# Late modulation vectors as VectorE dot products, and feed-forward transfers in program order, in a fused transformer block

## The chip, the cores and the metric

The kernel runs on one core of a Trainium2 chip (trn2). The metric is the device time of one execution in microseconds. The kernel before took 1283.59 us (median of 3 runs, 1283.0 to 1285.08).

## The reference, cut to what matters

```python
mod = (silu(c) @ w_mod).reshape(1, 6, 1, 1024)        # w_mod is 1024 x 6144, bf16
sa, ca, ga, sb, cb, gb = ...                           # six vectors of 1024
h = layernorm(x) * (1 + ca) + sa                       # x is 2048 x 1024
x = x + ga * attention(h)                              # 32 heads of 128, window of 512 keys, wq, wo
h = layernorm(x) * (1 + cb) + sb
x = x + gb * (silu(h @ w_gate) * (h @ w_up)) @ w_down  # feed-forward width 3584
```

`sa` and `ca` are needed at once. The other four vectors are needed later: `ga` and `gb` as rows that are the same in all partitions, `cb` and `sb` as columns (one value per partition). These four are the "late modulation vectors".

## The kernel before

The program is a list of 128 head steps (4 chunks of 512 rows, 32 heads each), with small tasks hung on the steps by `at(k, ...)`, and then the feed-forward (FFN) stage. A scheduler orders each engine's instructions; `pin` holds an instruction to program order. `fetch` and `load` issue all transfers from one queue, that of SyncE (SPq).

The late vectors were made on TensorE, two vectors at a time. The stationary side is silu(c), widened to 32 equal columns:

```python
sil32 = const.tile([P, DT, 32], BF16, name="sil32")
for dt in range(DT):                                   # eight VectorE fills, in the startup
    nc.vector.tensor_scalar(out=sil32[:, dt, :], in0=ones_bf[:, 0:32],
                            scalar1=siluc[:, dt:dt + 1], scalar2=None, op0=ALU.mult)

def mod_rows(n, part):                                 # runs at steps 5, 13, 21 and 29
    ps = mm("row_ps")
    tiles = [wm_rows.pop(0) for _ in range(2)]
    for k in range(4):
        for i in range(4):
            nc.tensor.matmul(ps[32 * i:32 * i + 32, :], lhsT=sil32[:, 4 * part + k, :],
                             rhs=tiles[i // 2][:, k, (i % 2) * 512:(i % 2 + 1) * 512],
                             start=(k == 0), stop=(k == 3))
    # ... VectorE adds the two parts and the result goes to DRAM as row_d

def load_cols(n, k, dst, add_one):                     # cb1 at step 16
    src = row_d[n][k:k + 2, :].rearrange("a (b p) -> p (a b)", p=P)
    with nc.allow_non_contiguous_dma(reason="1024 values to columns"):
        fetch(out=dst, in_=src)
    if add_one:                                        # VectorE, waits for that load
        nc.vector.tensor_scalar(out=dst, in0=dst, scalar1=1.0, scalar2=None, op0=ALU.add)
```

In the FFN stage transfers are not pinned, so the scheduler may order them freely:

```python
stage.update(dma=False, steps=False)
for cc in range(NTC):
    for fg in range(NFG):
        if (cc, fg) != (0, 0):
            load_gu(cc, fg)                            # gate and up tiles of this group
        if cc > 0:
            load_wd(cc, 0, fg)
        # ... emit_gu and the remaining tasks
    # ... down projection; its wd tiles are loaded in front of it
```

## Time and profile before

| | before |
|---|---|
| time, median of 3 | 1283.59 us |
| span of the profiled run | 1283.0 us |
| TensorE (PE) busy | 1270.0 us, 99% |
| VectorE (DVE) busy | 577.3 us, 45% |
| DMA queue of SyncE | 54.1% of 16 engines |

The first lines of the profile page of the kernel before; each engine line is busy time, share of the span, and instructions.

```profile
span 1283.0 us, 18137 instructions
PE 1270.0 (99%) x7601; PEld 643.1 (50%) x7601; DVE 577.3 (45%) x1271; ACT 333.9 (26%) x433; POOL 1.2 (0%) x8
```

TensorE hardly rests, so only work taken off it, or one of its few waits, can shorten the run. The groups view of the kernel before shows the two kinds of work that the change trades. Its columns are line, engine, operation, tiles and shapes, count; then busy time in us and mean ns of one; then idle time before.

```profile
L779 PE MATMUL row_ps<-wmr,sil 128*32 128x512 bf16 x64 | 4.2, 382 | 0.0
L955 DVE SCALAR_TENSOR_TENSOR junk<-wq 128x1024 bf16<-128x1024 bf16 x32 | 38.9, 1215 | 0.0
L955 DVE DVE_READ_ACCUMULATOR junk<-wq 128x1 f32 x32 | 2.6, 82 | 0.0
```

The 64 narrow matmuls occupy TensorE for 4.2 us together, although each record is 382 ns long. The timeline of TensorE shows one group of 16 (start, duration, instruction):

```profile
46.55 1.05 PE L779 MATMUL row_ps<-wmr,sil 128*32 128x512 bf16 x16
```

It takes 1.05 us, where 16 ordinary 128x512 matmuls at 0.216 us would take 3.46 us. The second and third lines of the groups view are a dot product that the kernel already does elsewhere: 1215 + 82 ns for 128x1024.

Four lines of the waits view of the kernel before turn out to matter. Columns: who waited, on whom; us in total, times, longest.

```profile
DVE modT L802 <- DMA modT<-row_d: 3.6, 1, 3.6
PE a_ps L1096 <- DVE acc L1102: 1.0, 1, 1.0
PE gu_ps L1173 <- DVE guT L1179: 0.8, 1, 0.8
PE mod_ps L753 <- DMA wm<-in_w_mod_dram: 1.7, 1, 1.7
```

The third stands in the FFN stage, and the fourth is TensorE waiting in the startup for a load of `w_mod`; both come back below. The first two belong together. This is VectorE in the timeline of the kernel before, from 86 to 94 us (start, duration, instruction; in brackets the idle time before it and what ended it):

```profile
87.84 0.54 DVE L835 TENSOR_SCALAR xn<-x,mv 128x1024 bf16<-128x1024 bf16 x1
92.00 0.17 DVE L802 TENSOR_SCALAR modT<-modT 128x8 f32<-128x8 f32 x1 [3.62 <-DMA modT<-row_d]
92.08 0.69 DVE L816 BATCH_NORM_STATS2 st<-x 128x6 f32<-128x512 bf16 x1
92.69 0.67 DVE L1102 COPY acc<-a_ps 128x512 f32<-128x512 f32 x1
```

And this is the chain of waits of the kernel before across the same time (start, duration, what):

```profile
86.93 5.05 DMA modT<-row_d
...
92.77 0.60 DVE acc L1102
...
93.41 1.89 PE a_ps L1096 x8
```

The `+ 1` on the cb columns (L802) stands in VectorE's order and waits 3.6 us for a 4 KB load that took 5.05 us. The accumulator copy behind it (L1102) comes late, and TensorE's next `a_ps` group waits for it.

### The profile page before, as it was taken

What the parts mean: (1) busy time and instruction counts of PE and PEld (TensorE: products, weight loads), DVE (VectorE), ACT (ScalarE), POOL (GpSimd) and SP (SyncE); (2) the same over time, 40 slices, a digit from 0 to 9 for tenths busy, and PEclk for the clock granted to TensorE, in tenths of its full rate; (3) what the DMA queues carried; (4) which work ended last, traced back from release to release, by engine and by line L of the source; (5) the groups of instructions that cost most, each with busy time, mean ns of one, the idle gap of its engine ahead of it and who ended that gap; (6) DMA issues with size and microseconds to landing.
All of it is one profiled execution on the core that took longest, in us unless ns stands there. A gap on an engine that the chain in (4) does not pass through costs nothing.

```text
span 1283.0 us, 18137 instructions
## 1 busy us (share of the span) xinstructions
PE 1270.0 (99%) x7601; PEld 643.1 (50%) x7601; DVE 577.3 (45%) x1271; ACT 333.9 (26%) x433; POOL 1.2 (0%) x8
## 2 busy tenths in 40 slices
PE   8999999999999999999999999999999999999998
PEld 4555555555555555555554444444444444444444
DVE  4464557865577755576663642221212221221122
ACT  3543334343333433333341111011100111011100
POOL 0000000000000000000000000000000000000000
PEclk8999999999999999999999999999999999999999
DMA  9878566557355554445678484454536455454401
GB/s 286 275 187 234 169 149 171 133 142 204 98 124 156 148 140 148 116 149 131 132 195 247 129 249 149 139 189 147 180 103 218 140 164 164 135 193 134 129 22 47
DMA packets 280108, 204.21 MB, mean 159 GB/s; under 512 B 113865, under 2 KB 273609, under 8 KB 280018
## 3 DMA queue, kind: packets, MB, share of 16 engines
q1 hardware_dynamic: 275106, 198.78, 54.1%
q10 hardware_dynamic: 4912, 4.20, 1.0%
q8 instruction: 61, 1.00, 0.3%
q14 instruction: 29, 0.24, 0.1%
HBM read 174.08 MB, written 4.21 MB: 139 GB/s over the span
## 4 chain that ended last, share of the span: by engine, by line
PE 96%; DMA 2%; DVE 1%; SPq 0%; ACT 0%; issue 0%; DVEq 0%
PE gu_ps L1173 29%; PE a_ps L1096 17%; PE q_ps L1019 17%; PE d_ps L1193 15%; PE o_ps L1064 9%; PE s_ps L1032 8%; DMA wm<-in_w_mod_dram 1%; DMA hT<-xn 1%; PE q_ps L940 0%; DMA modT<-row_d 0%; PE row_ps L779 0%; SPq L664 0%; PE mod_ps L753 0%; DVE st L816 0%; ACT pT L1034 0%; PE h_ps L927 0%
## 5 line engine op out<-in xcount | busy, mean ns | idle before, releaser
L1034 ACT ACTIVATE pT<-s_ps 128x1024 bf16<-128x1024 f32 x256 | 248.7, 1020 | 341.8 <-PE s_ps L1032 341.8
L1096 PE MATMUL a_ps<-wo,oT 128*128 128x512 bf16 x1024 | 241.9, 379 | 1.0 <-DVE acc L1102 1.0
L1019 PE MATMUL q_ps<-hT,wq 128*128 128x512 bf16 x1000 | 236.7, 379 | 0.3 <-DVE modT L755 0.3
L1173 PE MATMUL gu_ps<-hT,wg 128*128 128x512 bf16 x896 | 211.7, 379 | 0.8 <-DVE guT L1179 0.8
L1179 DVE TENSOR_TENSOR guT<-gu_ps,sg 128x512 bf16<-128x512 f32 x112 | 77.4, 691 | 282.5 <-ACT sg L1178 282.5
L1178 ACT ACTIVATE sg<-gu_ps 128x512 bf16<-128x512 f32 x112 | 66.9, 597 | 489.6 <-PE gu_ps L1173 438.4
L1193 PE MATMUL d_ps<-wd,guT 128*128 128x512 bf16 (+2 forms) x952 | 194.2, 366 | 0.0
L916 DVE CAST qT<-q_ps 128x512 bf16<-128x512 f32 x128 | 88.2, 691 | 176.9 <-PE q_ps L1019 176.3
L1173 PE MATMUL gu_ps<-hT,wu 128*128 128x512 bf16 x672 | 163.3, 379 | 0.0
L1096 PEld LDWEIGHTS <-oT 128*128 128x128 bf16 x1024 | 99.9, 98 | 122.3 <-issue 2.1
L1019 PEld LDWEIGHTS <-wq 128*128 128x128 bf16 x1000 | 97.8, 98 | 117.8 <-issue 0.3
L1193 PEld LDWEIGHTS <-guT 128*128 128x128 bf16 x952 | 90.9, 98 | 103.0
L1064 PEld LDWEIGHTS <-pT 128*128 128x128 bf16 x2048 | 126.6, 98 | 30.6 <-issue 0.4
L1173 PEld LDWEIGHTS <-wg 128*128 128x128 bf16 x896 | 87.6, 98 | 106.5 <-issue 1.1
L1064 PE MATMUL o_ps<-v_sb,pT 128*128 128x130 bf16 x2048 | 137.1, 220 | 0.0
L1032 PE MATMUL s_ps<-qT,kT 128*128 128x512 bf16 x512 | 131.5, 379 | 0.6 <-ACT pT L1034 0.6
L1173 PEld LDWEIGHTS <-wu 128*128 128x128 bf16 x672 | 65.8, 98 | 79.3
L1051 DVE TENSOR_TENSOR oq<-o_ps,rl 128x256 bf16<-128x256 f32 (+2 forms) x256 | 101.2, 419 | 4.3
L1197 DVE TENSOR_TENSOR f<-d_ps,gb_bc 128x512 f32<-128x512 f32 (+2 forms) x34 | 22.4, 660 | 147.1 <-PE d_ps L1193 147.1
L1104 DVE TENSOR_TENSOR acc<-a_ps,acc 128x512 f32<-128x512 f32 x64 | 44.0, 688 | 38.8 <-PE a_ps L1096 38.8
L1032 PEld LDWEIGHTS <-kT 128*128 128x128 bf16 x512 | 44.9, 98 | 31.7 <-issue 1.3
L1173 PE MATMUL gu_ps<-hT,v_sb 128*128 128x512 bf16 x224 | 57.5, 379 | 0.0
(77 smaller groups left out, 372.6 us busy)
## 6 DMA issues: line engine op xcount, KB each, us to landing
wq<-in_A_wq_dram SPq DMA_DIRECT2D x64, 512.0 KB, 4.2
wo<-in_A_wo_dram SPq DMA_DIRECT2D x64, 512.0 KB, 5.7
wg<-in_B_w_gate_dram SPq DMA_DIRECT2D x56, 512.0 KB, 4.5
wd<-in_B_w_down_dram SPq DMA_DIRECT2D x56, 512.0 KB, 7.1
wu<-in_B_w_up_dram SPq DMA_DIRECT2D x42, 512.0 KB, 5.9
wmr<-in_w_mod_dram SPq DMA_DIRECT2D x8, 1024.0 KB, 11.5
v_sb<-in_B_w_up_dram SPq DMA_DIRECT2D x14, 512.0 KB, 6.2
x<-in_A_x_dram SPq DMA_DIRECT2D x16, 256.0 KB, 5.7
```

The source lines that it names most:

```text
L916: nc.vector.tensor_copy(out=t, in_=q_ps)
L1019: nc.tensor.matmul(q_ps, lhsT=wq_tiles[(cc, h // 4, dt // 4)][:, dt % 4, (h % 4) * P:(h % 4 + 1) * P], rhs=hT[("h1", cc)][:, dt, :], start ...
L1032: nc.tensor.matmul(s_ps[:, i, :], lhsT=kT[:, kv, j * P:(j + 1) * P], rhs=qT[g], start=True, stop=True)
L1034: nc.scalar.activation(out=p[:, 2 * jj:2 * jj + 2, :], in_=s_ps, func=ACT.Exp, scale=scale)
L1051: nc.vector.tensor_tensor(out=dst, in0=ps[:, s0:s0 + cnt, 0:Dh], in1=sc, op=ALU.mult)
L1064: nc.tensor.matmul(o_slot["ps"][:, s_, :], lhsT=pT[g][:, j, t * P:(t + 1) * P], rhs=v_sb[:, kv, j, 0:VN], start=(j == 0), stop=(j == WT - 1))
L1096: nc.tensor.matmul(a_ps, lhsT=oT[(cc, 2 * q + i)][:, hh % 4, t * P:(t + 1) * P], rhs=wo_tiles[(cc, q, dh, i)][:, hh % 4, :], start=(hh == ...
L1104: nc.vector.tensor_tensor(out=acc[(cc, t)][:, dsl], in0=a_ps, in1=acc[(cc, t)][:, dsl], op=ALU.add)
L1173: nc.tensor.matmul(ps[:, n, :], lhsT=gu_w[(cc, fg, nm, dt // 4)][:, dt % 4, fi * P:(fi + 1) * P], rhs=hT[("h2", cc)][:, dt, :], start=(dt ...
L1178: nc.scalar.activation(out=g, in_=ps[:, 0, :], func=ACT.Silu)
L1179: nc.vector.tensor_tensor(out=guT[(cc, fg)][:, fi, :], in0=ps[:, 1, :], in1=g, op=ALU.mult)
L1193: nc.tensor.matmul(d_ps, lhsT=guT[(cc, f // 4)][:, f % 4, t * P:(t + 1) * P], rhs=wd_tiles[(cc, dh, f // 4)][:, f % 4, c0:c0 + w], start=( ...
```

## The change

Each late vector is computed on VectorE. Columns of `w_mod` are loaded by a transposing DMA (128 columns x 1024 rows per load), so that a vector element is the dot product of one partition's row with silu(c), which is spread over all partitions once (`c_bc`). There are 32 such tiles, one every second head step. The 64 narrow matmuls, the fills of `sil32`, the row loads, and the column load with its `+ 1` go. In the FFN stage the transfers are pinned to program order, and the next group's gate and up tiles are asked for before the wd tiles.

```diff
-    sil32 = const.tile([P, DT, 32], BF16, name="sil32")
-    for dt in range(DT):
-        nc.vector.tensor_scalar(out=sil32[:, dt, :], in0=ones_bf[:, 0:32],
-                                scalar1=siluc[:, dt:dt + 1], scalar2=None, op0=ALU.mult)
     # ... (load_rows, mod_rows, load_gate, load_cols removed)
+    c_d = dp.tile([DT, P], BF16, name="c_d", tag="c_d", bufs=1)
+    c_bc = const.tile([P, D], BF16, name="c_bc")
     # ...
+    def load_wmT(vec, j):
+        if j % 4 == 0:
+            wm_cols[(vec, j // 4)] = hpool.tile([P, 4, D], BF16, name="wmT", tag="hT")
+        c0 = vec * D + j * P
+        pin(nc.sync.dma_start_transpose(out=wm_cols[(vec, j // 4)][:, j % 4, :],
+                                        in_=w_mod[:, c0:c0 + P]), "dma")
+
+    def mod_dot(vec, j, dst):
+        t = wm_cols[(vec, j // 4)]
+        junk = wk.tile([P, D], BF16, name="junk", tag="junk", bufs=1)
+        pin(nc.vector.scalar_tensor_tensor(out=junk, in0=t[:, j % 4, :], scalar=1.0, in1=c_bc,
+                                           op0=ALU.mult, op1=ALU.mult,
+                                           accum_out=dst[:, j:j + 1]))
     # ... (add_one, store_gate with a 32x32 transposition, load_gate)
+    at(0, spread_c)
+    for vec, dst, starts in ((2, gcol[0], (1, 9)), (4, cb1, (17, 25)), (3, sb, (33, 41)),
+                             (5, gcol[1], (51, 61))):
         for part in range(2):
+            for i in range(4):
+                at(starts[part] + 2 * i, load_wmT, vec, 4 * part + i)
+                at(starts[part] + 2 * i + 3, mod_dot, vec, 4 * part + i, dst)
     # ...
-    stage.update(dma=False, steps=False)
+    stage.update(steps=False)
     for cc in range(NTC):
         for fg in range(NFG):
-            if (cc, fg) != (0, 0):
-                load_gu(cc, fg)
+            n = cc * NFG + fg + 1
+            if n < NTC * NFG:
+                load_gu(*divmod(n, NFG))
             if cc > 0:
                 load_wd(cc, 0, fg)
+            elif fg >= NFG - 4:
     # ... (two wd tiles per group; dh == 0 is no longer loaded in front of the down projection)
```

More of the change, by code (lines that the diff above doesn't have):

```diff
@@ L756, in mod_cols @@
                                 scalar1=1.0 if add_one else 0.0, scalar2=None, op0=ALU.add)
-    sil32 = const.tile([P, DT, 32], BF16, name="sil32")
-    for dt in range(DT):
-        nc.vector.tensor_scalar(out=sil32[:, dt, :], in0=ones_bf[:, 0:32],
-                                scalar1=siluc[:, dt:dt + 1], scalar2=None, op0=ALU.mult)
-    wm_rows = []
-    row_part = []
-    row_d = {}
-    def load_rows(vec, part):
-        t = hpool.tile([P, 4, D], BF16, name="wmr", tag="hT")
-        load(t, wm_v[:, 4 * part:4 * part + 4, vec * D:(vec + 1) * D])
-        wm_rows.append(t)
@@ L774, in mod_rows @@
-    def mod_rows(n, part):
-        ps = mm("row_ps")
-        tiles = [wm_rows.pop(0) for _ in range(2)]
-        for k in range(4):
-            for i in range(4):
-                nc.tensor.matmul(ps[32 * i:32 * i + 32, :], lhsT=sil32[:, 4 * part + k, :],
-                                 rhs=tiles[i // 2][:, k, (i % 2) * 512:(i % 2 + 1) * 512],
-                                 start=(k == 0), stop=(k == 3))
-        if part == 0:
-            r = blkC("row", [P, TCW], FP32)
-            nc.vector.tensor_copy(out=r, in_=ps)
-            row_part.append(r)
-        else:
-            r = row_part.pop()
-            nc.vector.tensor_tensor(out=r, in0=ps, in1=r, op=ALU.add)
-            d = dp.tile([4, TCW], FP32, name="row_d", tag="row_d", bufs=2)
-            fetch(out=d, in_=r[0:P:32, :])
-            row_d[n] = d
@@ L793, in load_gate @@
-    def load_gate(n, k, dst):
-        fetch(out=dst.rearrange("p (a b) -> p a b", a=2),
-                          in_=row_d[n][k:k + 2, :].partition_broadcast(P))
-    def load_cols(n, k, dst, add_one):
-        src = row_d[n][k:k + 2, :].rearrange("a (b p) -> p (a b)", p=P)
-        with nc.allow_non_contiguous_dma(reason="1024 values to columns"):
-            fetch(out=dst, in_=src)
-        if add_one:
-            nc.vector.tensor_scalar(out=dst, in0=dst, scalar1=1.0, scalar2=None, op0=ALU.add)
+    c_d = dp.tile([DT, P], BF16, name="c_d", tag="c_d", bufs=1)
@@ new lines, in fast_path, with spread_c @@
+    c_bc = const.tile([P, D], BF16, name="c_bc")
+    gcol = [const.tile([P, 32], FP32, name=f"gcol{n}") for n in range(2)]
+    grow = const.tile([P, 32], FP32, name="grow")
+    for n in range(2):
+        nc.gpsimd.memset(gcol[n], 0.0)
+    wm_cols = {}
+    col_d = {}
+    def spread_c():
+        fetch(out=c_d, in_=sil_r)
+        fetch(out=c_bc.rearrange("p (a b) -> p a b", a=DT), in_=c_d.partition_broadcast(P))
+    def load_wmT(vec, j):
[4 more added lines that the diff above has]
+                                        in_=w_mod[:, c0:c0 + P]), "dma")
@@ new lines, in mod_dot, with add_one, store_gate @@
+    def mod_dot(vec, j, dst):
[4 more added lines that the diff above has]
+                                           accum_out=dst[:, j:j + 1]))
+    def add_one(dst):
+        pin(nc.vector.tensor_scalar(out=dst, in0=dst, scalar1=1.0, scalar2=None, op0=ALU.add))
+    def store_gate(n):
+        d = dp.tile([DT, P], FP32, name="col_d", tag="col_d", bufs=2)
+        pin(nc.vector.transpose(out=grow, in_=gcol[n]))
+        for q in range(4):
+            fetch(out=d[:, 32 * q:32 * q + 32], in_=grow[32 * q:32 * q + DT, :])
+        col_d[n] = d
@@ L804, in fast_path, with load_gate @@
+    def load_gate(n, dst):
+        fetch(out=dst.rearrange("p (a b) -> p a b", a=DT), in_=col_d[n].partition_broadcast(P))
     tasks = {}
@@ L1111, in emit_wo @@
             nc.vector.tensor_tensor(out=x1, in0=f, in1=x1, op=ALU.add)
-    for n, vecs in enumerate(((2, 4), (5, 3))):
+    at(0, spread_c)
+    for vec, dst, starts in ((2, gcol[0], (1, 9)), (4, cb1, (17, 25)), (3, sb, (33, 41)),
+                             (5, gcol[1], (51, 61))):
         for part in range(2):
-            k = 16 * n + 8 * part
-            at(k, load_rows, vecs[0], part)
-            at(k + 2, load_rows, vecs[1], part)
-            at(k + 5, mod_rows, n, part)
-        at(16 * n + 15, load_gate, n, 0, gb_bc if n else ga_bc)
-        at(16 * n + 16, load_cols, n, 2, sb if n else cb1, n == 0)
+            for i in range(4):
+                at(starts[part] + 2 * i, load_wmT, vec, 4 * part + i)
+                at(starts[part] + 2 * i + 3, mod_dot, vec, 4 * part + i, dst)
+        k = starts[1] + 10
+        if vec == 4:
+            at(k, add_one, cb1)
+        elif vec in (2, 5):
+            at(k, store_gate, vec // 5)
+            at(k + 3, load_gate, vec // 5, gb_bc if vec == 5 else ga_bc)
     for tt in range(QT, S // P):
@@ L1220, in fast_path @@
             emit_o(k - 1)
-    stage.update(dma=False, steps=False)
+    stage.update(steps=False)
     for cc in range(NTC):
         for fg in range(NFG):
-            if (cc, fg) != (0, 0):
-                load_gu(cc, fg)
+            n = cc * NFG + fg + 1
+            if n < NTC * NFG:
+                load_gu(*divmod(n, NFG))
             if cc > 0:
                 load_wd(cc, 0, fg)
+            elif fg >= NFG - 4:
+                for i in range(2):
+                    if 2 * (fg - NFG + 4) + i < NFG:
+                        load_wd(0, 0, 2 * (fg - NFG + 4) + i)
             for fi in range(4):
@@ L1231, in fast_path @@
         for dh in range(DH):
-            if dh > 0 or cc == 0:
+            if dh > 0:
                 for fg in range(NFG):
```

## The prediction

> **What bounds the kernel.** TensorE. The page gives PE busy 1270.0 of 1283.0 us (99%) at a granted clock of 0.997. In the stretches view PE is busy 128.00 of 128.00 us from 128 us on, in every attention stretch, and 97.00 of 97.00 in the feed-forward (FFN) stretches. In the chain of waits, runs of eight 128x512 matmuls take 1.73 us, 0.216 us each, back to back. PE idles only at the start (5.8 us of the first 32), at the end (5.4 us), and 1.0 + 0.8 us elsewhere. VectorE is at 45%, the DMA engines at about 54%. So only work taken off PE, or those few idle microseconds, can shorten the run.
>
> **Removed.** 64 row_ps matmuls. Each record is 382 ns, but the groups view shows 4.2 us busy for all 64: 16 take 1.05 us, not 16 x 0.216 = 3.5. That agrees with the Trainium skill, "TensorEngine Tiling (Array Packing)", Performance Considerations, which allows up to 4x for a 32-wide stationary side. So PE gets back four pieces of about 1.05 us: **-4.2 us**, all on the critical path. Also gone: 4 evictions (0.69 us) and 8 fills (1.2 us) on VectorE, 8 MB of 1 MB row loads, four of them in the first 100 us, where the DMA share is 0.83 to 1.01.
>
> **Added.** 32 VectorE dot products of 128x1024 bf16. The same form (wq squares) takes 1215 + 82 ns, so 41.5 us, over the first 70 of 128 head steps. VectorE is busy about 112 of 170 us in the attention stretch and has slack in each step (1.3 us per two steps of 3.5 to 5.2 us): 0 us. 32 crossbar transposes of 256 KB: an SBUF transpose of 128 KB issues in 1.26 us and lands in 2.5 us; my estimate is 4 to 7 us to landing. Each dot stands three steps (10 to 16 us) behind its load, so it should not wait, except perhaps the first ones: the write and read-back of c blocks the DMA queue for a round trip at about 27 to 33 us, and the next wq tiles come behind it, needed at about 44.7 us. Estimate 0 to +1 us.
>
> **Moved.** The order view shows PE's order unchanged but for the missing matmuls and one startup swap (second mod_ps group behind two transposition groups): within 0.5 us. FFN transfers now stand in program order: the next gate/up tiles are asked for before wd. There are as many buffers, so four gate/up tiles still come in the 13.8 us of a tile group; PE waits for no transfer in that stage before, so nothing can be won: 0 us. The one 0.8 us PE wait for VectorE's guT at 755.9 us may vanish or return elsewhere.
>
> **Sum.** 1283.6 - 4.2 - 0.4 (part of the small waits) + 0.4 (early queue round trip) = **1279.4 us**, range **1277.0 to 1284.0**. Faster by over 2%: 0.01; within 2%: 0.96; slower by over 2%: 0.03.
>
> **What would show it.** Right: row_ps gone; PE about 1266 us busy, still 99%; VectorE up about 38 us, to some 615; ga_bc and modT arriving before use; no DMA among the causes of PE waits after 50 us; FFN stretches as long as before. Wrong on dot products: VectorE idle before the dot line with the wmT transfer named, and PE idle behind qT or oq. Wrong on the queue: PE waiting for wq or wo, or for wg, wu, wd.
>
> **What would make it wrong.** Transposes from DRAM with 256-byte rows landing much more slowly than 7 us: VectorE in program order then stalls and holds PSUM from PE. A program-ordered transfer (an hT transpose waiting for VectorE, or a wd tile waiting for a buffer) blocking the gate/up tiles behind it: several us per chunk. A different startup clock: about 1 us either way.

## The result, and the profile after

The changed kernel took 1276.94 us (median of 6 runs, 1275.89 to 1277.89), the kernel before 1284.17 us (6 runs). The ratio is 0.9943, with a 95% interval of 0.993 to 0.9956. Ratios here are the mean time of one kernel's runs over the mean of the other's from the same rounds, so they are not quite the ratio of the medians. This is a clear 7.2 us by medians, where 4.2 us were predicted. It lies 0.06 us below the predicted range.

The first lines of the page of the changed kernel:

```profile
span 1275.6 us, 17906 instructions
PE 1255.9 (98%) x7396; PEld 640.6 (50%) x7537; DVE 606.9 (48%) x1325; ACT 333.7 (26%) x433; POOL 1.3 (0%) x10
```

Some matmul records are missing from this trace (7396 against 7537 weight loads), so its PE busy time is a little low. VectorE's busy time is up 29.6 us, less than the 38 us that the prediction expected. That is a matter of counting: the lengths of all its records add up to 630.2 us before and 668.0 us after, which is 37.9 us more (41.6 us of dot products, less 4.5 us of fills and evictions, and small changes), but records overlap in time, and the busy time counts an overlap once. The groups view of the changed kernel has the dot products as estimated, with no idle time in front of them:

```profile
L786 DVE SCALAR_TENSOR_TENSOR junk<-wmT,c_bc 128x1024 bf16<-128x1024 bf16 x32 | 38.9, 1216 | 0.0
L786 DVE DVE_READ_ACCUMULATOR junk<-wmT,c_bc 128x1 f32 x32 | 2.7, 83 | 0.0
```

VectorE in the timeline of the changed kernel at the corresponding place, 83 to 89 us:

```profile
83.47 0.54 DVE L834 TENSOR_SCALAR xn<-x,mv 128x1024 bf16<-128x1024 bf16 x1
84.59 0.69 DVE L1101 COPY acc<-a_ps 128x512 f32<-128x512 f32 x1 [0.58 <-PE a_ps L1095]
```

The load that it stood behind is gone, and the accumulator is copied 0.58 us after VectorE became free. Neither TensorE's wait for `acc` nor its wait for `guT` is in the waits view any more.

Where do the 7.4 us between the two profiled spans (1283.0 and 1275.6 us) come from? I followed the same VectorE evictions (its copies of finished matmul results) through both traces. An eviction follows its matmul group, so where VectorE itself is not late, its shift is TensorE's shift:

| stretch | eviction that closes it: before, after (us) | shift gained here |
|---|---|---|
| startup, to the fifth `qT` eviction on VectorE | 33.29, 31.08 | -2.21 |
| four places where `row_ps` was | -1.08, -1.08, -1.08, -1.09 | -4.33 |
| at 88 to 94 us of the kernel before (the `acc` wait) | 98.83, 93.31 | -1.15 |
| rest of attention | 681.44, 674.05 | +0.30 |
| at 751 to 757 us (the `guT` wait) | 800.1, 791.72 | -0.99 |
| last eviction to the end of the span | | +1.0 |

The four `row_ps` places are as predicted. The other 3 us were booked as zero in the prediction. The last row is particular to this one execution: from the last eviction to the end of the span it took 6.3 us here, and 5.1 to 5.3 us in all other 17 profiles of this case.

The startup row needs its own view. Stretches view, kernel before and then changed kernel: from:to and length, busy us of PE, PEld, DVE, ACT, POOL, then granted TensorE clock, DMA share, GB/s.

```profile
0.00:28.00 28.00, 22.78 (x217) 12.50 (x218) 13.31 (x44) 8.95 (x16) 1.23 (x8) 0.88 1.01 279
8.00:16.00 8.00, 5.32 (x94) 4.06 (x95) 4.77 (x20) 3.17 (x8) 0.00 (x0) 0.80 1.10 354
```

```profile
0.00:28.00 28.00, 22.29 (x222) 11.81 (x225) 13.87 (x38) 11.26 (x19) 1.35 (x10) 1.00 0.99 295
8.00:16.00 8.00, 5.92 (x105) 4.30 (x107) 3.74 (x12) 3.61 (x9) 0.00 (x0) 1.00 1.09 384
```

Two things differ before any changed transfer is issued: the clock (0.88 against 1.00), and the rate of the same loads (354 against 384 GB/s), at a full DMA share in both. The first score matmul falls at 27.7 us before and 25.1 us after. TensorE's wait for the load of `w_mod`, 1.7 us before, is shorter in the waits view of the changed kernel:

```profile
PE mod_ps L753 <- DMA wm<-in_w_mod_dram: 0.5, 1, 0.5
```

### The profile page after: what moved, and what is told of

Its sections match the earlier page's. It is cut to its first block, busy times and chain, and to the rows that moved or that the text cites. A ratio compares the mean times of both kernels' runs of the same rounds, so it can differ in the third digit from the quotient of the medians.

```text
span 1275.6 us, 17906 instructions
## 1 busy us (share of the span) xinstructions
PE 1255.9 (98%) x7396; PEld 640.6 (50%) x7537; DVE 606.9 (48%) x1325; ACT 333.7 (26%) x433; POOL 1.3 (0%) x10
## 4 chain that ended last, share of the span: by engine, by line
PE 96%; SPq 2%; issue 1%; DVE 1%; DMA 0%
PE gu_ps L1177 30%; PE a_ps L1095 17%; PE q_ps L1018 17%; PE d_ps L1197 15%; PE o_ps L1063 9%; PE s_ps L1031 8%; SPq L664 1%; SPq L703 1%; DMA wq<-in_A_wq_dram 0%; DVE junk L954 0%; DVE qT L915 0%; DVE junk L786 0%; DVE acc L1103 0%; DVE oq L1050 0%; DVE f L1201 0%
```

## The experiments

Kernels named b_ are edits of the kernel before, a_ of the changed kernel. All results were correct. Four submissions, each with its own runs of the kernel before on its chip; "mean change" is the mean of a kernel's runs less the mean of those.

| submission | kernel | median, us | mean change, us | first score matmul, us | clock, 0 to 28 us | GB/s, 8 to 16 us |
|---|---|---|---|---|---|---|
| 1 (before 1284.09) | b_fills_late | 1284.99 | +0.6 | 27.2 | 0.94 | 348 |
| | a_fills_back | 1276.81 | -7.4 | 25.8 | 0.94 | 386 |
| | a_mod_first | 1276.33 | -7.9 | 25.6 | 0.94 | 386 |
| | b_warm | 1285.72 | +1.7 | 31.1 | 0.84 | 354 |
| 2 (before 1284.78) | b_pad | 1282.62 | -2.2 | 25.5 | 0.94 | 386 |
| | a_pad | 1277.71 | -7.1 | 27.0 | 0.94 | 350 |
| | b_cols_late | 1282.99 | -2.0 | 25.9 | 0.94 | 352 |
| | b_ffn_new | 1283.32 | -1.8 | 27.1 | 0.94 | 356 |
| 3 (before 1284.20) | a_again (changed kernel) | 1277.27 | -6.8 | 26.4 | 0.94 | 386 |
| | a_rows_back | 1280.87 | -2.9 | 25.1 | 1.00 | 385 |
| | b_all_but_dots | 1281.05 | -3.2 | 25.1 | 1.00 | 386 |
| | a_dots_twice | 1277.68 | -5.8 | 27.0 | 0.94 | 382 |
| 4 (before 1285.14) | a_third (changed kernel) | 1275.96 | -8.9 | 25.2 | 1.00 | 385 |
| | a_pad2 (= a_pad) | 1278.30 | -7.3 | 26.0 | 1.00 | 350 |
| | b_cols_ffn | 1282.33 | -3.1 | 27.4 | 0.88 | 352 |
| | a_wq_before_v | 1275.84 | -9.5 | 25.1 | 1.00 | 386 |

A 95% interval of a time against the kernel before is about +-2.2 us in submission 1 and +-1.7 us in the others. The gains of b_pad, b_cols_late and b_ffn_new are just clear of zero by it, and time alone ranks no two neighbours here; shifts in the traces carry the finer statements. These shifts are taken against the one kept profile of the kernel before (or of the changed kernel, where it says so). It was run at another time. The changed kernel itself, run three times as a_again, a_third and in the first result, was 6.8 to 8.9 us below the kernel before of its chip.

### First theory for the startup: the fills and the clock

The fills of `sil32` stand in VectorE's startup order. In the kernel before they delay the statistics of the third x tile by 1.2 us; the built programs show that the scheduler then puts both first `mod_ps` groups ahead of the third transposition group. TensorE idles 1.7 us (in the waits view, for the load of `w_mod`), and its clock is halved for a while after. My theory was that this was the startup's 2 to 2.6 us.

b_fills_late, from the kernel before:

```diff
-    for dt in range(DT):
-        nc.vector.tensor_scalar(out=sil32[:, dt, :], ...)
+    def fill_sil():
+        for dt in range(DT):
+            pin(nc.vector.tensor_scalar(out=sil32[:, dt, :], ...))
...
+    at(1, fill_sil)
```

> The kernel before, with only its eight small VectorE fills of sil32 moved out of the startup to head step 1. Theory S (the fills delay the row statistics of the third x tile; TensorE then finds a gap and reorders, and its clock is halved for some 6 us): first score matmul at 25.1 to 25.6 us instead of 27.7, granted clock of the first 28 us near 1.00 instead of 0.88, time 2.0 to 2.6 us shorter (about 1281.8). Rival R (the startup gain of the changed kernel comes from its lighter early row loads or from chance in the clock): first score matmul still near 27.7 us, time unchanged.

Measured: 1284.99 us against 1284.09; first score matmul 27.2 us; loads at 348 GB/s. The evictions of attention gained 0.3 us and no more.

a_fills_back, from the changed kernel (dead fills; the order of TensorE's startup becomes exactly that of the kernel before):

```diff
+    sil32 = const.tile([P, 4, 32], BF16, name="sil32")
+    for dt in range(DT):
+        nc.vector.tensor_scalar(out=sil32[:, dt % 4, :], ...)
     c_d = dp.tile([DT, P], BF16, name="c_d", tag="c_d", bufs=1)
```

> The changed kernel with eight VectorE fills (dead data) put back where they stood in the startup; the build shows that the order of the matmuls there becomes that of the kernel before. Theory S: first score matmul back at about 27.7 us, clock of the first 28 us near 0.88, time 2.0 to 2.6 us longer than the changed kernel (about 1279.2). Rival R: first score matmul stays near 25.1, time unchanged (about 1276.9).

Measured: 1276.81 us, as the changed kernel; first score matmul 25.8 us; loads at 386 GB/s.

a_mod_first, from the changed kernel: the first two `mod_cols` calls moved ahead of the third tile, with these matmuls and the transpositions pinned.

```diff
     for t in range(QT):
+        if t == 2:
+            mod_cols(1, 0, ca1, True)
+            mod_cols(0, 0, sa, False)
         ln_stats(t)
```

> The changed kernel with the matmuls of the startup pinned in the order of the kernel before (both mod_ps groups ahead of the third transposition group), but without the fills. If the order alone opens the gap on TensorE: first score matmul 26.5 to 27.7 us, clock below 0.95 in the first 28 us, time 1.5 to 2.6 us longer. If the fills' 1.2 us on VectorE is what counts and the order only follows from it: first score matmul 25.1 to 25.6, time within 0.5 us of the changed kernel.

Measured: 1276.33 us; first score matmul 25.6 us, as in a_fills_back.

b_warm, from the kernel before:

```diff
-        warm(2)
+        warm(8 if t == 1 else 2)
```

> The kernel before with eight instead of two idle-filling matmuls after the second transposition group; VectorE and its fills untouched. If the halved clock is the cost and the gap its cause: clock of the first 28 us near 1.00, first score matmul 25.3 to 26.3 us, time 1.5 to 2.4 us shorter than the kernel before. If the delay of the row statistics is the cost and the clock only a sign: first score matmul at 27.0 us or later, time within 0.7 us of the kernel before, clock or no clock.

Measured: 1285.72 us (1284.11 to 1288.56). The clock stayed high to 16 us and was low from there on, and the first score matmul came at 31.1 us in the profiled run, the slowest of the four. Filling the gap did not keep the clock.

So the theory fell. The order and the fills together move the startup by at most 0.3 to 0.7 us, and the time by nothing that the runs resolve. A dip of the clock to about half speed falls at a varying place of the startup in 12 of the 18 profiles of this case (those with a clock below 1.00 over the first 28 us). The unedited changed kernel has it too: its three profiles show 1.00, 0.94 and 1.00. The 0.88 of the first profile pair was therefore partly chance.

What did separate the kernels cleanly was the last column of the table: 348 to 356 GB/s in some, 382 to 386 in the others, whatever the order or the clock.

### Second theory: where the load targets stand in SBUF

The addresses in the built programs show a side effect of the change. `sil32` went and `c_bc` and a few small tiles came, so that every buffer behind them moved. The first `wm` tile stands at byte 65664 of each partition in the kernel before, 128 past a multiple of 256, and at 67584 in the changed kernel, on a multiple. In a_fills_back it is at 67840, also on one, and in b_fills_late and b_warm at 65664. The tile sizes in the diff agree: per partition `sil32` took 512 bytes, and `c_bc`, the two `gcol` and `grow` take 2048 + 256 + 128, so everything behind them moves by 1920 bytes. The Trainium skill, "DMA: Bandwidth & Descriptors", section "How a descriptor splits into AXI transactions", says that a descriptor that does not start on a 256-byte boundary costs extra bus beats. For a 1 KB piece that starts 128 bytes past one, its counting gives 36 beats instead of 32; that is an estimate from this page, 12% more. The page speaks of bytes that are fetched; that the same count holds for the target of a load is my assumption.

b_pad, from the kernel before (and a_pad is the same two lines in the changed kernel, where they move the targets off the boundary, to 67712):

```diff
+    pad = const.tile([P, 64], BF16, name="pad")
+    nc.gpsimd.memset(pad, 0.0)
     sil32 = const.tile([P, DT, 32], BF16, name="sil32")
```

> The kernel before, with nothing but an unused 128-byte tile in front, so that every load target in SBUF stands at a multiple of 256 bytes (65792 instead of 65664, which is 128 past one). Theory A (the startup loads are the startup's limit and run at 348 GB/s when their targets are off a 256-byte boundary, at 385 when on one): 380 to 390 GB/s from 8 to 16 us, first score matmul 25.4 to 26.2 us instead of 27.7, time 1.5 to 2.2 us shorter (about 1282.2). Rival (the faster startup comes with something else in the changed kernel): 348 GB/s, 27.2 to 27.7 us, time unchanged.

Measured: 1282.62 us against 1284.78. Stretches view of b_pad:

```profile
8.00:16.00 8.00, 6.75 (x107) 4.69 (x107) 5.01 (x20) 3.71 (x10) 0.00 (x0) 0.88 1.09 386
```

The rate is that of the changed kernel, with fills, order and all else of the kernel before. First score matmul at 25.5 us. The evictions of attention are 1.9 to 2.0 us earlier than in the profile of the kernel before. (The `guT` wait happens to be missing in this profile too, which is another 1.0 us of it.)

> The changed kernel with an unused 128-byte tile in front, so that its load targets stand 128 bytes past a multiple of 256 (67712 instead of 67584). Theory A: 345 to 352 GB/s from 8 to 16 us, first score matmul 26.5 to 27.5 us instead of 25.1, time 1.4 to 2.4 us longer than the changed kernel (about 1278.8). Rival: 385 GB/s, 25.1 us, time unchanged.

Measured: 350 GB/s, first score matmul 27.0 us, 1277.71 us. The rate and the startup did as expected; the time was not clearly longer than that of the changed kernel, which had been measured on another chip. So it was repeated beside it:

> The changed kernel, unedited, as partner on the same chip of a_pad2 and a_wq_before_v. Expected 1276.3 to 1277.7 us.

> a_pad again, this time beside the changed kernel on one chip. If load targets off a 256-byte boundary cost time and not only bandwidth: 0.6 to 1.6 us longer than a_third, most likely 1.0, with 350 GB/s from 8 to 16 us against 385. If the bandwidth is lost in waiting that nothing depends on: within 0.4 us of a_third.

Measured: 1278.30 us against 1275.96 of a_third; the means are 1278.07 and 1276.54, 1.5 us apart. Stretches view of a_pad2 and of a_third:

```profile
8.00:16.00 8.00, 5.89 (x106) 4.25 (x107) 3.74 (x13) 3.79 (x9) 0.00 (x0) 1.00 1.10 350
```

```profile
8.00:16.00 8.00, 5.94 (x106) 4.26 (x107) 3.74 (x12) 3.65 (x9) 0.00 (x0) 1.00 1.09 385
```

The wait of TensorE for `w_mod` in the waits view, again of a_pad2 and of a_third:

```profile
PE mod_ps L753 <- DMA wm<-in_w_mod_dram: 1.1, 1, 1.1
```

```profile
PE mod_ps L753 <- DMA wm<-in_w_mod_dram: 0.5, 1, 0.5
```

That the rate follows the alignment is shown, in both directions, by an edit that does nothing else; only places 0 and 128 bytes past a multiple of 256 were tried. The wait for `w_mod` follows it too: 1.1 to 2.1 us in all eight profiles with targets off the boundary, 0 to 1.0 us in all ten with targets on it, with means 0.9 us apart.

What it is worth in time is known less well. Over all profiles but b_warm, the first score matmul comes at 26.9 us in the mean of seven with targets off the boundary and at 25.6 us in the mean of ten with targets on it, 1.3 us apart. But the clock dip is mixed into this: six of the seven have it, and five of the ten. Among profiles of equal clock over the first 28 us the difference is 0.9 us (clock 1.00: one profile against five) and 0.7 us (0.94: four against five). The times of a_pad2 and a_third agree: their runs with a mean clock of 1.000 are 0.9 us apart and those with 0.998 are 1.0 us apart, with one to four runs on each side. So the alignment is worth about 0.7 to 1.0 us at an equal clock. Whether it also makes a dip more likely is open.

### The two waits

b_cols_late, from the kernel before:

```diff
-        if add_one:
-            nc.vector.tensor_scalar(out=dst, in0=dst, scalar1=1.0, scalar2=None, op0=ALU.add)
+    def add_one(dst):
+        pin(nc.vector.tensor_scalar(out=dst, in0=dst, scalar1=1.0, scalar2=None, op0=ALU.add))
...
-        at(16 * n + 16, load_cols, n, 2, sb if n else cb1, n == 0)
+        at(16 * n + 16, load_cols, n, 2, sb if n else cb1)
+    at(26, add_one, cb1)
```

> The kernel before, with the one VectorE addition that waits for the cb1 columns moved from head step 16 to step 26. Theory C (VectorE stood 3.6 us behind that load in program order and held an accumulator from TensorE): that wait of VectorE gone, TensorE's 1.0 us wait for acc gone, time 0.9 to 1.2 us shorter (about 1283.0). Rival: the wait moves to another place and the time stays.

Measured: 1282.99 us against 1284.78. In the trace VectorE's wait for `modT` and TensorE's for `acc` are gone (the one for `guT` is not touched, and stays at 0.6 us), and the evictions shift by 1.15 us exactly there (from -1.40 to -2.55 us against the kernel before). The 1.40 us ahead of that is the startup of this run (clock 0.94 against 0.88), which the edit does not touch: a lucky draw that makes the time look better than the cause.

b_ffn_new, from the kernel before, has the FFN part of the change alone:

```diff
-    stage.update(dma=False, steps=False)
+    stage.update(steps=False)
...
-            if (cc, fg) != (0, 0):
-                load_gu(cc, fg)
+            n = cc * NFG + fg + 1
+            if n < NTC * NFG:
+                load_gu(*divmod(n, NFG))
... (and the wd tiles of the first chunk, as in the change)
```

> The kernel before, with the FFN transfers in the program order of the changed kernel and nothing else. Theory F (the free order bunched the last row transpositions, so eight affine steps stood in front of two guT products at 754 to 757 us): TensorE's wait for guT gone, time 0.8 to 1.1 us shorter (about 1283.1). Rival, as predicted: 0, the wait comes back elsewhere.

Measured: 1283.32 us against 1284.78. The shift of the evictions goes from -0.40 us in attention to -1.39 us in the first down projection, so -0.99 us there, and the wait of TensorE for `guT` is gone. In the kernel before, VectorE had run eight affine steps in two bunches around that product, as its timeline from 752 to 757 us shows:

```profile
753.84 1.38 DVE L856 TENSOR_SCALAR hT<-hT,modT 128x512 bf16<-128x512 bf16 x4 [2.66 <-DMA hT<-xn]
755.14 0.68 DVE L1179 TENSOR_TENSOR guT<-gu_ps,sg 128x512 bf16<-128x512 f32 x1
755.74 1.37 DVE L856 TENSOR_SCALAR hT<-hT,modT 128x512 bf16<-128x512 bf16 x4
```

In program order the last transposed load comes later, and with it the affine steps. How often the wait comes in the kernel before is not settled: it was there in the profiles of the kernel before, b_fills_late, b_warm and b_cols_late (0.6 to 1.0 us), and not in that of b_pad. The bunches alone do not bring it: b_pad has the same two, 0.4 us earlier against the `guT` products than in the kernel before.

### The narrow matmuls, and the whole remainder

a_rows_back, from the changed kernel; dead work, the outputs stay right (the fourth group stands at step 27, where the kernel before had it at 29):

```diff
+    def dead_rows(cc):
+        ps = mm("row_ps")
+        for k in range(4):
+            for i in range(4):
+                nc.tensor.matmul(ps[32 * i:32 * i + 32, :], lhsT=sil32[:, k, :],
+                                 rhs=hT[("h1", cc)][:, k, :], start=(k == 0), stop=(k == 3))
+        r = blkC("row", [P, TCW], FP32)
+        nc.vector.tensor_copy(out=r, in_=ps)
...
+    for k in (5, 13, 21, 27):
+        at(k, dead_rows, 0)
```

> The changed kernel with the 64 narrow matmuls put back as dead work, in four groups of 16 at the steps where the kernel before had them, each evicted once by VectorE. If what they cost is their place on TensorE: 1.05 to 1.15 us a group, 4.2 to 4.6 us in all, time 1281.1 to 1281.6. If they cost less because TensorE had slack there: under 2 us. If more (mode changes on TensorE beyond what the records show): over 6 us.

b_all_but_dots joins b_pad, b_fills_late, b_cols_late and b_ffn_new in one kernel:

> The kernel before, with the 128-byte tile in front, the fills out of the startup, the addition behind the cb1 columns moved to step 26, and the FFN transfers in program order: all that changed but the modulation vectors' way of being computed. If the gain splits as 4.4 us for the narrow matmuls and the rest for these side effects: 2.6 to 3.2 us shorter than the kernel before (about 1281.3), equal to a_rows_back within 0.7 us. If the single gains measured apart (2.2, 1.8 and 1.5 us) add up: 5.0 to 5.8 us shorter (about 1279).

> The changed kernel once more, unedited, as the partner on the same chip of the three runs beside it. Expected 1276.3 to 1277.5 us, 7.2 us below the kernel before; 385 GB/s from 8 to 16 us. A startup dip of the clock may come in this profile, where the first one had none: then the first score matmul falls at 25.5 to 26 us instead of 25.1, and so a part of the 2.6 us by which the first two profiles differ there is chance.

Measured, on one chip: changed kernel 1277.27, a_rows_back 1280.87, b_all_but_dots 1281.05, kernel before 1284.20 us. The evictions of a_rows_back shift by 1.08, 1.08, 1.08 and 1.10 us at the four places, 4.3 us in all, and by 3.9 us in the mean time. The two kernels in the middle were reached from opposite ends, and their means differ by 0.2 us. The sum closes within 0.3 us: 3.9 us for the narrow matmuls and 3.2 us for everything else, against 6.8 us measured between the ends. The single gains (2.2 + 2.0 + 1.8 us) do not add up to these 3.2 us: by their traces, each held some of the startup's luck or of the `guT` wait.

b_cols_ffn joins only b_cols_late and b_ffn_new, with the startup untouched:

> The kernel before with the addition behind the cb1 columns moved and the FFN transfers in program order, but its load targets still 128 bytes past a 256-byte boundary and its fills in the startup. If the two TensorE waits (1.15 us for acc, 0.8 to 1.0 us for guT) are what these two parts are worth: 1.7 to 2.3 us shorter than the kernel before, which leaves some 1 us of the 3.2 us of b_all_but_dots for the startup. If the startup is worth nothing in the mean: 2.8 us or more shorter.

Measured: 1282.33 us against 1285.14; 3.1 us by the means, more than the two waits were expected to give, with a kernel before that scattered more on this chip (1283.31 to 1287.48). In the trace the evictions end 2.45 us earlier than in the profile of the kernel before, 0.31 of it in the startup, so 2.1 us for the two waits. The time thus speaks for a startup that is worth nothing, and the trace against it. The times cannot decide this. Measured from the kernel before, b_all_but_dots gains only 0.1 us more than b_cols_ffn; measured from the changed kernel on the same chip, b_cols_ffn is 5.8 us slower and b_all_but_dots 3.6 us, which would leave 2.1 us for the startup.

### Is VectorE's added work free?

a_dots_twice, from the changed kernel, does each dot product twice; the outputs stay right:

```diff
-        pin(nc.vector.scalar_tensor_tensor(out=junk, in0=t[:, j % 4, :], ...))
+        for _ in range(2):
+            pin(nc.vector.scalar_tensor_tensor(out=junk, in0=t[:, j % 4, :], ...))
```

> The changed kernel with each of the 32 VectorE dot products done twice (41.5 us more VectorE work, result unchanged). If VectorE has slack in these steps, as predicted: within 0.5 us of the changed kernel. If the dot products already cost something on TensorE's path: at least 1 us longer, with TensorE waiting for acc, oq or qT between 40 and 380 us.

Measured: 1277.68 us against 1277.27, and 1.0 us longer in the mean. Against the first profile of the changed kernel its evictions are 1.56 us late out of the startup and 3.05 us late after step 70, so the second set of dot products cost 1.5 us, with waits such as `o_ps` for `oq` (0.9 us). This is the second case: VectorE has no room for a second set. One set is nearly free: the changed kernel lost 0.3 us over that stretch. a_rows_back, which has the dot products, lost the same 0.3 us there, and b_all_but_dots, which has none, lost nothing.

### A faster version

The changed kernel reached its second head group early enough to wait for that group's wq tiles at 28.5 us (0.25 us in its own profile, 0.4 us in that of a_rows_back). a_wq_before_v moves `load_wq(0, 1)` ahead of the V loads:

```diff
+    load_wq(0, 1)
     for kv in range(Hkv):
         load(v_sb[:, kv, :, 0:Dh], v_v[:, kv])
     nc.gpsimd.memset(v_sb[:, :, :, Dh:VN], 1.0)
-    load_wq(0, 1)
```

> The changed kernel with the second head group's wq tiles asked for before the V tiles, because TensorE waited about 0.4 us for wq at 28.5 us in its profile. If that wait is real and V comes early enough: 0.3 to 0.5 us shorter than a_third and no wait of q_ps for a wq transfer. Rival: the wait moves to V (o_ps) and the time stays.

Measured: 1275.84 us against 1275.96; 0.7 us less by the means, which the runs do not separate. In the trace no q_ps matmul waits for a wq transfer, and the evictions after the startup are 0.8 us earlier than in a_third. But a_third's profile has no such wait either, so its removal is not where these 0.8 us come from. What a_third has and this kernel has not are two waits of score matmuls for ScalarE's `pT` (0.25 us at 26.9 us and 0.32 us at 27.8 us); here q_ps matmuls of the second group stand in these gaps. Another 0.1 us is there at the first score matmul already. It is the fastest kernel, by a little.

## Why the prediction was right or wrong

- **"Removed ... -4.2 us, all on the critical path": right.** Putting the matmuls back cost 3.9 us in the mean time and 4.3 us in the trace. The Trainium skill, "TensorEngine Tiling (Array Packing)", Performance Considerations, allows up to 4x for a 32-wide stationary side; a group of 16 took 1.08 us against 16 x 0.216 = 3.46 us, which is 3.2x.
- **"Added. 32 VectorE dot products ... 0 us": right within 0.3 us.** Their duration was 1216 + 83 ns. None waited for its transposed load, although a load had only three steps of time. The slack was smaller than the prediction took it to be: a second set of dot products cost 1.5 us in the trace.
- **"Estimate 0 to +1 us" for the round trip of c: right in that it cost nothing visible.** The read-back was issued at 28.7 us, and no TensorE wait follows from it. The + 0.4 us for it in the sum did not appear.
- **"Moved ... FFN: 0 us": wrong by about 1 us.** "The one 0.8 us PE wait for VectorE's guT at 755.9 us may vanish or return elsewhere" was the right place, but it did vanish.
- **"- 0.4 (part of the small waits)": the step that failed.** The two waits were worth about 2.1 us (1.15 for `acc`, 1.0 for `guT`). The `acc` wait should have been counted in full: the diff deletes the very load and the very addition that VectorE stood behind, and both were in the chain of waits.
- **Startup "within 0.5 us": wrong.** The first profiles differ by 2.2 us there. About 0.7 to 1.0 us of it is the load targets' alignment, which follows from the tile sizes in the diff (1920 bytes, not a multiple of 256) and not from the order of instructions. Most of the rest is the clock dip, which only one of the two profiles has; the prediction's "A different startup clock: about 1 us either way" was of the right size.

The mechanism named was right and clear of noise, and its term was sized well. The total was off because the remaining terms of the sum, -0.4 + 0.4 = 0, measured -3.2 us (b_all_but_dots): about -1.15 for `acc`, -1 for `guT`, and the remaining -1 for the startup. Those three numbers come from traces and are each good to some tenths of a microsecond. The startup's share is not shown by time alone (b_cols_ffn). The +1.0 us at the end of the first profile of the changed kernel is not part of this: in a_again the last eviction came 0.94 us later, and the span was still 0.3 us shorter.

Left open: why the clock dips in most startups and not in all; how often the kernel before meets the `guT` wait; and the split of the startup between alignment and order beyond the 0.3 to 0.7 us seen for the order.

## What to carry to other kernels

Where one engine is busy 99% of the time, list its few waits one by one and ask of each whether the diff deletes its cause; a removed load may free an engine that stood behind it in program order. Look up the addresses that a change gives to load targets: an unused 128-byte tile that moved them onto a 256-byte boundary made a DMA-limited startup load 9% faster (354 to 386 GB/s). And where effects are near a microsecond, join the parts from both ends (here a_rows_back and b_all_but_dots) rather than add up single gains.

## What the Trainium skill lacked or had wrong

- "DMA: Bandwidth & Descriptors", section "How a descriptor splits into AXI transactions", tells the cost in beats and for bytes that are fetched; it gives no rate and does not say that SBUF targets of loads are concerned. Here moving the targets by 128 bytes, with nothing else, changed 354 to 386 GB/s (b_pad, 8 to 16 us) and 385 to 350 (a_pad2), factors of 1.09 and 1.10, where its counting gives an estimate of 1.12.
- "SBUF — State Buffer", section "Operand start alignment", says of its measurements that they timed nothing. A sentence that 256-byte alignment of a load target matters for speed belongs there (same numbers).
- "DMA: Bandwidth & Descriptors", section "Where 436 GB/s comes from", says that about 358 GB/s bind a transfer between HBM and SBUF, and does not repeat there that this is the share of a core whose neighbour streams too, as the page's table of measurements just above it says. With one core running, 385 to 386 GB/s were held from 8 to 16 us, from HBM to SBUF.
- "TensorEngine Tiling (Array Packing)", section "Key Properties", says that a change of the tiling mode drains TensorE and gives no cost. A group of 16 narrow matmuls, entered from and left to the full array, cost 1.08 us; 16 x 0.216 / 4 = 0.86 us would be without any, so at most about 0.2 us for both changes together (an estimate from these two numbers; another cause of the difference was not excluded).
